# Two program jumps moved to the ends, LayerNorm roots on VectorE instead of ScalarE, and one MLP input taken off GpSimd

## The chip, the cores and the metric

The kernel runs on one core of one Trainium2 chip. The metric is the time of the whole program on the device, in microseconds (us), lower is better. The kernel before takes 1396.98 us (median of 3 runs, 1396.61 to 1397.05).

Words used here: TensorE does the matmuls, VectorE and ScalarE the elementwise work (VectorE also moves results out of PSUM, such as those of the matmuls with V, in 256 operations of line 755: an eviction), GpSimd helps, and SyncE issues data transfers, as ScalarE can too. In profile lines these are PE, DVE, ACT, POOL and SP; a q behind a name (ACTq, SPq) marks transfers issued by that engine. PSUM is the memory that the matmuls write. The granted clock is the share of TensorE's full clock that the trace shows as granted; a half-clock spell is a stretch in which it is 0.5. A milestone is the start of the same matmul in several traces.

## The reference, cut to what matters

```python
mod = (silu(c) @ w_mod).reshape(..., 6, 1, -1);  sa, ca, ga, sb, cb, gb = mod...
h = layernorm(x) * (1 + ca) + sa
x = x + ga * A(h)          # A: q = h @ wq; softmax(q k^T / sqrt(128)) v; @ wo
h = layernorm(x) * (1 + cb) + sb
x = x + gb * B(h)          # B: layernorm, gelu(@ w1), shifts, @ w2, + h; layernorm, gelu(@ w3) @ w4, + x1
# x: 2048 x 640; 32 heads of 128, 2048 cached keys and values per head; w_mod 640 x 3840
# w1, w2: 640 x 640; w3: 640 x 1728; w4: 1728 x 640; all bf16
```

## The kernel before: the parts that matter

The rows are cut into four chunks of 512, counted 0 to 3 in the code. Attention is 128 steps (8 groups of 4 heads, in each group 4 chunks of 4 heads). A step is 16 score matmuls (line 727), exps on ScalarE (729), 16 times 4 matmuls with V (746), and the projection of the next step's q (659). After 128 steps comes a tail for the MLP.

A list scheduler in the kernel puts every operation into one list per engine by cost and priority; each engine then executes its own list strictly in order. So an operation that is late holds back what stands behind it on its engine (at the end of attention TensorE stood for 3.75 us behind one eviction, below). The program has a fast path and a general path, which runs only if a check fails. Each engine runs a few operations, then jumps over the general path to the rest of its list:

```python
    FIRST = {"PE": 3, "ACT": 5, "DVE": 0, "POOL": 7, "SP": 7}   # operations ahead of the jump
...
        for e, eng in names.items():
            hint = eng.mark_branch_hint_location()
            run(e, 0, self.FIRST[e])
            eng.br("fast").branch_hint(hint)
        es.close()
        general()
        nc.switch_bb("fast")
        for e, eng in names.items():
            run(e, self.FIRST[e], None)
```

The first LayerNorm, with roots on ScalarE (Ln, then Exp of -0.5 times it), and the loads of heads:

```python
    def ln1(ch, prio):
        g = ln_slot()
        xs = x0 if ch == 0 else load_x2(...) + load_x2(...)
        for a in (0, 2):
            for i in (a, a + 1):
                ln_stats(xs[i].ap, (xs[i],), g, i, prio, 0.0 if ch == 0 else 2000.0)
            rstd_act(g, a, a + 2, prio - 100, 0.0 if ch == 0 else 1500.0)
            for i in (a, a + 1):
                normed(xn[i].ap, xn[i], xs[i].ap, xs[i], g, i, False, prio - 1)
        # ... cut: the transposes, on TensorE for chunk 0, by transfers for the others
    def load_head(h):
        # ... cut: b, n, pr
        load_k(h, pr, (wm[2],) if h == 1 else (), from_slot(n))       # 4 transposing transfers
        load_v(h, pr + 1, gate=(wm[2],) if h == 1 else (), need=from_slot(n + 1))
```

The tail is a list of pieces in the order TensorE executes them. A is a part of w1, B a tile of w2, C a part of w3, D a tile of w4, WO the last output projection of attention, I3 the MLP input (the double LayerNorm) of chunk 3:

```python
    TAIL = ("A0 B0 B1 B2 A1 B3 WO B4 B5 A2 B6 I3 B7 B8 C0 B9 D0 D1 ... ").split()
    WOD, CH, I3D = -200, -300, 0     # VectorE priorities: evictions of WO, rest of the tail, I3
...
    def mlp_in(ch, prio):
        for a in (0, 2):
            pool = ch < NC - 2 or (ch == NC - 2 and a == 0)      # half of chunk 2 on GpSimd
            # rstd: ScalarE if pool, else eight tiny Newton operations on VectorE
            ...
                if pool:
                    scaled("POOL", ...); tt("POOL", ... mod_t[4] ...); tt("POOL", ... mod_t[3] ...)
                else:
                    P.op("DVE", ... scalar_tensor_tensor(x1 - mean, times mod_t[4]) ...)
```

## Time and profile before

| what | value |
|---|---|
| time, median | 1396.98 us |
| profiled span | 1396.2 us, mean granted clock 0.995 |
| TensorE busy | 1382.3 us, 99% |
| first q projection starts | 16.40 us |
| last step of attention gives way to the tail (A0) | 1208.68 us |

TensorE is busy nearly all the time, so the change can only work on what TensorE loses. From the page of the kernel before, the busy line, and then the shares of the chain that ended last:

```profile
PE 1382.3 (99%) x13128; PEld 942.0 (67%) x13128; DVE 539.8 (39%) x1380; ACT 1106.6 (79%) x1164; POOL 110.4 (8%) x96
...
PE 97%; DVE 2%; issue 1%; DMA 0%; SPq 0%; ACT 0%; ACTq 0%; POOL 0%; POOLq 0%
```

TensorE's own waits (columns: engine, tile and line that waited, what it waited for; total us, how often, the longest), the largest ones:

```profile
PE f_O L857 <- DVE f_OO L755: 3.7, 1, 3.7
PE f_O L553 <- DVE f_xn L510: 1.5, 2, 0.9
...
PE f_M L445 <- DMA f_W<-in_w_mod_dram: 0.6, 2, 0.3
PE f_O L746 <- DMA f_KV<-in_A_v_cache_dram: 0.5, 1, 0.5
```

Two places stand out. The first is the start. ScalarE's timeline (start, busy time, engine, line, operation, output and input; in brackets the idle time before it and what ended it):

```profile
4.70 0.18 ACT L435 ACTIVATE f_small<-f_M 128x5 f32<-128x5 f32 x1
10.68 0.38 ACTq L612 DMA_DIRECT2D f_KV<-in_w_mod_dram  x1
11.10 0.54 ACTq L582 DMA_DIRECT2D f_KV<-in_A_v_cache_dram  x1
11.69 0.20 ACT L483 ACTIVATE f_small<-f_small 128x2 f32<-128x2 f32 x1 [6.81 <-issue]
```

ScalarE does nothing from 4.88 to 10.68 and waits for nothing that the profile shows: this is its jump. (The w_mod slice that its next load awaits landed only at 6.61, so the jump costs it about 4.1 us of these 5.8.) The first LayerNorm root (line 483) is late by that, and with it the first projection.

The second is the end of attention. VectorE's, GpSimd's and TensorE's timelines around it:

```profile
1203.49 1.48 DVE L496 SCALAR_TENSOR_TENSOR f_small<-f_small 128x2 f32<-128x2 f32 x1
1205.01 1.47 DVE L497 TENSOR_TENSOR f_small<-f_small 128x2 f32<-128x2 f32 x1
1206.51 1.47 DVE L498 SCALAR_TENSOR_TENSOR f_small<-f_small 128x2 f32<-128x2 f32 x1
1208.01 2.92 DVE L794 SCALAR_TENSOR_TENSOR f_y<-f_y,f_small,f_mod 128x640 f32<-128x640 f32 x2
...
1203.42 6.04 POOL L517 TENSOR_TENSOR f_y<-f_y,f_mod 128x640 f32<-128x640 f32 x4
...
1209.76 1.24 PE L857 MATMUL f_S<-f_wq,f_W 128*128 128x512 bf16 x5
1214.75 2.32 PE L857 MATMUL f_O<-f_wq,f_W 128*128 128x512 bf16 x5 [3.75 <-DVE f_OO L755]
```

Operations on 128 by 2 numbers, of 0.15 to 0.17 us elsewhere, take about as long as one of the GpSimd operations beside them (6.04 / 4 = 1.51 us). VectorE is late, TensorE waits 3.75 us for an eviction, and the next five matmuls take 2.32 us instead of 1.24, at half clock. Busy times in windows, with the granted clock behind the engines' columns (DMA share and GB/s last), for the two places:

```profile
15.00:20.00 5.00, 4.36 (x19) 1.98 (x17) 2.27 (x6) 1.45 (x2) 0.00 (x0) 0.51 1.36 183
...
1215.00:1220.00 5.00, 5.00 (x13) 1.82 (x12) 3.87 (x16) 1.20 (x2) 0.00 (x0) 0.50 0.49 81
```

### The profile page before, as it was taken

To read this page: it belongs to the slowest core of one execution; us is meant where nothing else is said; L and a number is where in the kernel's file an instruction comes from. 1 tells how busy PE (TensorE), PEld (TensorE's weight loads), DVE (VectorE), ACT (ScalarE), POOL (GpSimd) and SP (SyncE) were. 2 spreads that over 40 slices of the span, in tenths; PEclk is the share of its full clock that TensorE was granted. 3 is DMA by queue.
4 is the path that set the end of the run, shared out by engine and by line. 5 is a ranking of instruction groups with operands and counts; after the bars stand their busy time and mean duration, and the time that the engine had idled before them with its cause. 6 is when DMAs were issued, how large, how long until landed. Compare 5 with 4: busy or idle time off the path is not lost.

```text
span 1396.2 us, 29870 instructions
## 1 busy us (share of the span) xinstructions
PE 1382.3 (99%) x13128; PEld 942.0 (67%) x13128; DVE 539.8 (39%) x1380; ACT 1106.6 (79%) x1164; POOL 110.4 (8%) x96
## 2 busy tenths in 40 slices
PE   8999999999999999999999999999999999899999
PEld 6667767677777777777776777777776676555554
DVE  4452332333233322333233323333233345887653
ACT  4988888888888898888888888888888888643222
POOL 0000000000000000000000000001333248300000
PEclk9999999999999999999999999999999999999999
DMA  9661623161214321241206112612254112432110
GB/s 207 138 119 25 121 76 86 35 107 36 46 35 81 61 46 35 50 92 31 50 19 97 32 42 35 107 35 47 54 103 102 16 16 53 93 70 38 39 48 24
DMA packets 259180, 88.90 MB, mean 64 GB/s; under 512 B 236706, under 2 KB 257763, under 8 KB 259043
## 3 DMA queue, kind: packets, MB, share of 16 engines
q1 hardware_dynamic: 255762, 84.59, 30.8%
q10 hardware_dynamic: 3280, 2.33, 0.6%
q8 instruction: 105, 1.72, 0.6%
q14 instruction: 33, 0.26, 0.1%
HBM read 43.48 MB, written 2.62 MB: 33 GB/s over the span
## 4 chain that ended last, share of the span: by engine, by line
PE 97%; DVE 2%; issue 1%; DMA 0%; SPq 0%; ACT 0%; ACTq 0%; POOL 0%; POOLq 0%
PE f_O L746 33%; PE f_S L727 31%; PE f_M L659 10%; PE f_M L684 10%; PE f_M L921 3%; PE f_O L907 2%; PE f_S L907 2%; PE f_S L921 2%; PE f_S L880 1%; PE f_O L857 1%; PE f_S L857 1%; PE f_M L880 1%; DMA f_KV<-in_A_v_cache_dram 0%; PE f_M L604 0%; PE f_S L420 0%
## 5 line engine op out<-in xcount | busy, mean ns | idle before, releaser
L729 ACT ACTIVATE f_PQ<-f_S 128x1024 bf16<-128x1024 f32 x1024 | 1041.2, 1023 | 147.0 <-PE f_S L727 133.8
L746 PEld LDWEIGHTS f_O<-f_KV,f_PQ 128*128 128x128 bf16 x8192 | 589.5, 98 | 232.3 <-DVE f_OO L755 2.2
L727 PE MATMUL f_S<-f_PQ,f_KV 128*128 128x512 bf16 x2048 | 727.9, 380 | 0.5 <-ACT f_PQ L729 0.5
L746 PE MATMUL f_O<-f_KV,f_PQ 128*128 128x129 bf16 x8192 | 713.7, 220 | 1.4 <-DVE f_OO L755 0.9
L692 DVE TENSOR_TENSOR f_y<-f_M,f_y 128x320 f32<-128x320 f32 x192 | 94.4, 492 | 536.3 <-PE f_M L684 536.3
L684 PE MATMUL f_M<-f_wo,f_OO 128*128 128x320 bf16 x992 | 273.3, 300 | 0.0
L727 PEld LDWEIGHTS f_S<-f_PQ,f_KV 128*128 128x128 bf16 x2048 | 196.9, 98 | 30.7 <-ACT f_PQ L729 1.0
L659 PE MATMUL f_M<-f_hT,f_wq 128*128 128x512 bf16 x640 | 177.4, 381 | 1.1 <-DVE f_hT L562 0.6
L517 POOL TENSOR_TENSOR f_y<-f_y,f_mod 128x640 f32<-128x640 f32 x36 | 55.6, 1557 | 820.1 <-DVE f_y L692 819.9
L684 PEld LDWEIGHTS f_M<-f_wo,f_OO 128*128 128x128 bf16 x992 | 96.1, 98 | 28.5
L755 DVE TENSOR_TENSOR f_OO<-f_O,f_rl 128x256 bf16<-128x256 f32 x256 | 108.5, 424 | 8.2
L662 DVE CAST f_PQ<-f_M 128x512 bf16<-128x512 f32 x128 | 88.5, 692 | 56.2 <-PE f_M L659 56.0
L659 PEld LDWEIGHTS f_M<-f_hT,f_wq 128*128 128x128 bf16 x640 | 62.2, 98 | 65.9 <-DVE f_hT L562 1.6
L753 DVE RECIPROCAL f_rl<-f_O 128x2 f32<-128x2 f32 x256 | 43.4, 170 | 32.4 <-PE f_O L746 28.2
L910 ACT ACTIVATE f_OO<-f_S 128x512 bf16<-128x512 f32 x28 | 16.7, 597 | 39.6 <-PE f_S L907 39.6
L690 DVE COPY f_y<-f_M 128x320 f32<-128x320 f32 x32 | 15.7, 490 | 62.4 <-PE f_M L684 62.4
L921 PE MATMUL f_M<-f_KV,f_OO 128*128 128x320 bf16 x252 | 38.6, 301 | 0.0
L921 PEld LDWEIGHTS f_M<-f_KV,f_OO 128*128 128x128 bf16 x252 | 23.2, 97 | 15.6 <-issue 6.0
L523 ACT ACTIVATE f_xn<-f_y,f_small 128x640 bf16<-128x640 f32 x10 | 9.1, 914 | 29.6 <-DVE f_small L502 29.6
L478 DVE BATCH_NORM_STATS2 f_small<-f_y 128x6 f32<-128x320 f32 x64 | 29.8, 479 | 2.0 <-POOL f_y L517 2.0
L921 PE MATMUL f_S<-f_KV,f_OO 128*128 128x320 bf16 x196 | 30.0, 301 | 0.0
L910 ACT ACTIVATE f_OO<-f_O 128x512 bf16<-128x512 f32 (+1 forms) x28 | 16.6, 594 | 12.0 <-PE f_O L907 12.0
(136 smaller groups left out, 521.1 us busy)
## 6 DMA issues: line engine op xcount, KB each, us to landing
f_KV<-in_A_v_cache_dram SPq DMA_DIRECT2D x31, 512.0 KB, 4.6
f_wo<-in_A_wo_dram SPq DMA_DIRECT2D x8, 640.0 KB, 4.3
f_xin<-in_A_x_dram SPq DMA_DIRECT2D x15, 320.0 KB, 3.6
f_wq<-in_A_wq_dram SPq DMA_DIRECT2D x7, 640.0 KB, 4.6
f_W<-in_w_mod_dram SPq DMA_DIRECT2D x3, 800.0 KB, 4.8
out_dram<-f_xin SPq DMA_DIRECT2D x15, 160.0 KB, 1.8
f_KV<-in_B_w_dram SPq DMA_DIRECT2D x5, 432.0 KB, 3.4
f_KV<-in_A_k_cache_dram SPq DMA_TRANSPOSE x128, 3.0
```

The lines of the kernel that those rows point to most:

```text
L517: P.op(eng, lambda e: e.tensor_tensor(out=out, in0=a, in1=b, op=op), COST[eng][0], rd, wr, prio, lat=300 if eng == "POOL" else None)
L659: P.op("PE", lambda e, i=i, kk=kk: e.matmul(m.ap, wq_t[g % 2][:, kk, hh * 128:(hh + 1) * 128], hT_t[ch][:, kk, :], start=(i == 0), stop=(i ...
L662: P.op("DVE", lambda e: e.tensor_copy(q.ap, m.ap), 690, (m,), (q,), s * NP - 90)
L684: P.op("PE", lambda e, m=m, qt=qt, hf=hf, hh=hh: e.matmul(m[:, 0:HD], OT_ap[gs][:, qt, hh, :], wo_t[g % 2][:, hh, hf * HD:(hf + 1) * HD], ...
L692: P.op("DVE", lambda e, m=m, yt=yt: e.tensor_tensor(out=yt.ap, in0=m[:, 0:HD], in1=yt.ap, op=ALU.add), 490, (m, yt), (yt,), s * NP - 60)
L727: P.op("PE", lambda e, sp=sp, r=r, kt=kt: e.matmul(sp[:, r * QC:(r + 1) * QC], K_ap[b][:, kt * 128:(kt + 1) * 128], q.ap, start=True, stop ...
L729: x = P.op("ACT", lambda e, sp=sp, pt=pt: e.activation(pt.ap.rearrange("p k q -> p (k q)"), sp.ap, ACT.Exp, scale=SCALE), 1021, (sp,), (pt ...
L746: ins = e.matmul(o[bk][:, w * 129:w * 129 + 129], pt[:, r, qt * 128:(qt + 1) * 128], V_ap[b][:, u, 0:129], start=(u == 0 and w == 0), stop ...
L753: P.op("DVE", lambda e, ov=ov, i0=i0: e.reciprocal(rl_t[:, i0:i0 + 2].unsqueeze(2), ov[:, 0:258].rearrange("p (u d) -> p u d", u=2)[:, :, ...
L755: evac.append(P.op("DVE", lambda e, ov=ov, i0=i0, bk=bk: e.tensor_tensor(out=On_ap[gs][:, 2 * bk:2 * bk + 2, hh, :], in0=ov[:, 0:258].rear ...
L907: P.op("PE", lambda e, m=m, f=f, kk=kk, fs=fs: e.matmul(m[0:fs, :], w3_ap[:, kk, f * 128:f * 128 + fs], nT_ap[ch][:, kk, :], start=(kk == ...
L921: P.op("PE", lambda e, f=f, hf=hf, fs=fs: e.matmul(m[:, hf * 512:hf * 512 + HD], gT_ap[0:fs, f, i * 128:(i + 1) * 128], w4_ap[f][0:fs, hf ...
```

## The change

The intent: ScalarE and SyncE no longer pay for their jump at the start; the roots of later chunks' first LayerNorm go to VectorE as Newton iterations, off the busy ScalarE; and the MLP input of chunk 2 (the third) no longer uses GpSimd, so that VectorE is not slowed at the end of attention. The tail's order and priorities are tuned anew.

```diff
-    FIRST = {"PE": 3, "ACT": 5, "DVE": 0, "POOL": 7, "SP": 7}
+    FIRST = {"PE": 3, "ACT": 10000, "DVE": 0, "POOL": 7, "SP": -5}
+    HINT = {"PE": 0, "ACT": -30, "DVE": 0, "POOL": 0, "SP": -12}
...
         for e, eng in names.items():
+            n = self.HINT[e] % len(self.seq[e])
+            run(e, 0, n)
             hint = eng.mark_branch_hint_location()
-            run(e, 0, self.FIRST[e])
+            run(e, n, self.FIRST[e])
             eng.br("fast").branch_hint(hint)
... ln1:
-        for a in (0, 2):
+        for a, z in ((0, 2), (2, 4)) if ch < 2 else ((0, 4),):
...
-            rstd_act(g, a, a + 2, prio - 100, 0.0 if ch == 0 else 1500.0)
+            if ch == 0:
+                rstd_act(g, a, z, prio - 100)
+            else:
+                rstd_dve(g, a, z, prio - 1)
... tail:
-    TAIL = ("A0 B0 B1 B2 A1 B3 WO B4 B5 A2 B6 I3 B7 B8 C0 B9 D0 D1 D2 D3 C1 D4 A3 B10 B11 "
-            "B12 B13 B14 D5 D6 D7 B15 C2 D8 D9 D10 D11 C3 D12 D13 D14 D15").split()
+    TAIL = ("A0 B0 B1 A1 B2 B3 WO B4 B5 I3 A2 B6 C0 B7 D0 D1 D2 B8 D3 B9 C1 D4 A3 B10 B11 "
+            "B12 D5 B13 D6 B14 D7 B15 C2 D8 D9 D10 D11 C3 D12 D13 D14 D15").split()
-    WOD, CH, I3D = -200, -300, 0
+    QUAD = (2, 3)
+    WOD, CH, I3D = -100, -1000, -200
... mlp_in:
-        for a in (0, 2):
-            pool = ch < NC - 2 or (ch == NC - 2 and a == 0)
+        pool = ch < NC - 2
+        for a, z in ((0, 4),) if ch in QUAD else ((0, 2), (2, 4)):
... (the rest follows from a, a + 2 becoming a, z, and cost entries 825 becoming 890)
```

More of the change, by code (lines that the diff above doesn't have):

```diff
@@ L536, in ln1 @@
         xs = x0 if ch == 0 else load_x2(4 * ch, XP[ch], from_slot(XS[ch])) + load_x2(4 * ch + 2, XP[ch], from_slot(XS[ch]))
-        for a in (0, 2):
-            for i in (a, a + 1):
+        for a, z in ((0, 2), (2, 4)) if ch < 2 else ((0, 4),):
+            for i in range(a, z):
                 ln_stats(xs[i].ap, (xs[i],), g, i, prio, 0.0 if ch == 0 else 2000.0)
-            rstd_act(g, a, a + 2, prio - 100, 0.0 if ch == 0 else 1500.0)
-            for i in (a, a + 1):
+            if ch == 0:
+                rstd_act(g, a, z, prio - 100)
+            else:
+                rstd_dve(g, a, z, prio - 1)
+            for i in range(a, z):
                 normed(xn[i].ap, xn[i], xs[i].ap, xs[i], g, i, False, prio - 1)
@@ L771, in rstd @@
                 if pool:
-                    rstd_act(g, a, a + 2, prio, 2000.0)
-                    negate(g, a, a + 2, prio, 2000.0)
-                else:
-                    rstd_dve(g, a, a + 2, prio)
-            for i in (a, a + 1):
+                    rstd_act(g, a, z, prio, 2000.0)
+                    negate(g, a, z, prio, 2000.0)
+                else:
+                    rstd_dve(g, a, z, prio)
+            for i in range(a, z):
                 t = ch * 4 + i
@@ L779, in mlp_in @@
             if not pool:
-                for i in (a, a + 1):
+                for i in range(a, z):
                     t = ch * 4 + i
@@ L783, in mlp_in @@
                         out=b.ap, in0=x1[t].ap, scalar=mv_ap[g1][:, i, 0:1], in1=mod_t[4][:], op0=ALU.subtract, op1=ALU.mult),
-                        825, (x1[t], mvs[g1][i]) + tuple(mod[4]), (xb[t],), prio)
+                        890, (x1[t], mvs[g1][i]) + tuple(mod[4]), (xb[t],), prio)
             rstd(g1)
-            for i in (a, a + 1):
+            for i in range(a, z):
                 t = ch * 4 + i
@@ L795, in mlp_in @@
                         out=b.ap, in0=b.ap, scalar=rs_ap[g1][:, i:i + 1], in1=mod_t[3][:], op0=ALU.mult, op1=ALU.add),
-                        825, (b, rs[g1]) + tuple(mod[3]), (b,), prio)
+                        890, (b, rs[g1]) + tuple(mod[3]), (b,), prio)
                 ln_stats(b.ap, (b,), g2, i, prio, 500.0)
@@ L799, in mlp_in @@
             if tail:
-                shift(g2, a, a + 2, prio)
-            for i in (a, a + 1):
+                shift(g2, a, z, prio)
+            for i in range(a, z):
                 t = ch * 4 + i
```

## The prediction

> **What bounds the kernel now.** TensorE: 99% busy on the page and 97% of the chain of waits. The change touches only the two ends, so I account for TensorE's lost time there.
>
> *Start.* The timeline shows ScalarE idle from 4.88 to 10.68 us; the chain of waits calls 5.92 us of it "issue". That is its jump after five operations; the w_mod slice that its next DMA awaits landed at 6.6. The delay holds the first LayerNorm root (11.69), so the first projection starts at 16.40. SyncE's jump delays the second K transpose to about 13.9, though its gate landed at 9.96. TensorE idles meanwhile, and the clock is halved from 15.1 to 21.9 (0.51 in the window 15 to 20). [...]
>
> *Tail.* At 1211.0 TensorE waits 3.75 us for a VectorE eviction (L755), its longest wait. VectorE was behind: tiny Newton operations took 1.48 us instead of 0.16, and L794 1.46 instead of 0.88, while GpSimd ran its 1.5 us tensor operations of chunk 2's MLP input (1203.4 to 1209.4). The gap cools the clock: half from 1213.1 to 1220.0, about 2.7 us of work lost (five matmuls take 2.3 us, not 1.24). [...]
>
> **What the change does.**
> 1. ScalarE issues its DMAs at 6.6, its first root about 8.1. Then wm slices, not ScalarE, bound TensorE: the third lands at 9.96 and now competes with 1.3 MB issued 4 us earlier. First projection about 14.8: 1.6 us gained. [...] Expected 2.8.
> 2. Roots by Newton cost VectorE eight operations of about 0.1 us per pair, off the critical path. The new order puts the eviction ahead of the cast that delayed TensorE at 32.3 to 33.4 (about 0.7), and the waits near 50 (0.7) mostly go. Expected 1.2.
> 3. Tail: no GpSimd beside VectorE, so the 3.75 us wait and its half clock go: 6.4. One GELU wait (0.28) goes.
> 4. Cost: VectorE takes two more tiles (about 4.6 us), repaid by the contention that ends. Step 126's eviction now stands behind four 0.8 us operations (about 0.5 lost), and the last output projection's evictions stand behind LayerNorm work, so its fifth and seventh groups should wait for PSUM, about 1.5 us against 0.45 before. A possible cold window there: 0.6 on average. Other slips 0.4. Together 2.6.
> 5. The late jumps: ScalarE's after its last GELU, SyncE's before the last five stores: hidden.
>
> Sum: 2.8 + 1.2 + 6.7 - 2.6 = 8.1 us. Predicted 1389, eight times in ten within 1384 to 1394. Faster by over 2%: 0.005; within 2%: 0.99; slower: 0.005.
>
> **What would show it.** Timeline: ScalarE's first Ln near 8, first projection near 14.8; clock row full at 15 to 25 or not (step 1's coin). TensorE's waits: no 3.75 us for L755; clock full at 1205 to 1225; Newton operations all near 0.15 us; a wait of 1 to 2 us in the last output projection. Middle steps unchanged.
>
> **What would make it wrong.** The early 1.3 MB delaying w_mod or K; the clock going cold anyway; a late jump landing on the end; the tail's VectorE queue holding back the first w3 tile.

The sum: 2.8 + 1.2 + 6.7 - 2.6 = 8.1 us. Cut from the forecast are two sentences that rest on general rules and not on a trace of this case, and in item 1 the sentence that took 1.6 to 2.8: the other 1.2 us were the author's estimate for a chance, put at 55%, that the half-clock spell at the start would stay away ("step 1's coin"). Without it the terms come to 6.9 us. A cold spell or cold window is a half-clock spell; its 0.6 in item 4 is a bet on its coming, like the 55%. The Newton operations of item 2, put there at about 0.1 us, take 0.11 to 0.17 us in the changed kernel (0.16 mostly; 28.06 to 33.8 us).

## The result, and the profile after

The changed kernel takes 1392.62 us (median of 4 runs, 1391.46 to 1392.70), where the kernel before took 1397.01 (1396.61 to 1398.72, 4 runs) in the same rounds. The ratio is 0.9964, 95% interval 0.9947 to 0.9982: the same within 2%. Ratios here and below are the mean time of one kernel's fast runs over the mean of the other's fast runs of the same rounds, so not quite the ratio of the medians. In means the kernel won 5.0 us (1397.34 to 1392.35), where the prediction had said 8.1.

The changed kernel's line numbers are 3 to 7 higher: 746 is now 753, 659 is 666, 684 is 691, 445 is 448, 755 is 762, 794 is 801. TensorE's waits after:

```profile
PE f_O L753 <- DMA f_KV<-in_A_v_cache_dram: 1.9, 1, 1.9
PE f_O L691 <- DVE f_tmp L702: 1.4, 1, 1.4
PE f_M L448 <- issue: 1.3, 1, 1.3
...
PE f_O L691 <- DVE f_small L500: 0.5, 1, 0.5
```

The wait of 3.7 us is gone; a wait for V of a head, 0.5 us before, is now 1.9; the last output projection (line 691) waits 2.0 us in all, 0.45 before; and there is a pause of 1.3 us marked issue. ScalarE at the start, and TensorE's pause as the chain of waits shows it:

```profile
7.18 0.39 ACTq L618 DMA_DIRECT2D f_KV<-in_w_mod_dram  x1
...
8.62 0.20 ACT L486 ACTIVATE f_small<-f_small 128x2 f32<-128x2 f32 x1 [3.21 <-DVE f_small L482]
...
11.91 0.13 PE f_M L448 x6
12.03 1.34 issue
13.38 0.25 PE f_M L448 x4
```

The jump is gone from ScalarE's start: its first root begins at 8.62 instead of 11.69. The tail's output projection, where TensorE now loses time (its timeline), and the clock there and at the start (windows):

```profile
1225.74 0.71 PE L691 MATMUL f_S<-f_wo,f_OO 128*128 128x320 bf16 x4
1227.88 0.72 PE L691 MATMUL f_O<-f_wo,f_OO 128*128 128x320 bf16 x4 [1.43 <-DVE f_tmp L702]
...
1229.67 1.25 PE L691 MATMUL f_O<-f_wo,f_OO 128*128 128x320 bf16 x4 [0.54 <-DVE f_small L500]
...
15.00:20.00 5.00, 5.00 (x20) 2.14 (x20) 2.37 (x5) 1.86 (x4) 0.13 (x1) 0.71 1.29 224
...
1230.00:1235.00 5.00, 5.00 (x28) 3.11 (x27) 2.99 (x11) 0.11 (x1) 0.00 (x0) 0.70 0.32 64
```

Where the time went is read best from milestones: the start times, in us, of the same matmuls in both traces.

| TensorE reaches | before | after | gain so far |
|---|---|---|---|
| first q projection | 16.40 | 14.85 | 1.55 |
| second | 22.84 | 20.26 | 2.58 |
| third | 31.02 | 28.44 | 2.58 |
| fourth | 39.94 | 36.61 | 3.33 |
| fifth | 48.11 | 44.91 | 3.20 |
| sixth | 57.57 | 55.84 | 1.73 |
| A0, first part of w1 | 1208.68 | 1207.44 | 1.24 |
| last output projection (WO) | 1232.30 | 1224.12 | 8.18 |
| A2, third part of w1 | 1239.98 | 1235.12 | 4.86 |
| D15, last tile | 1389.04 | 1384.17 | 4.87 |

(Up to WO and up to A2 TensorE does the same work in both, in a slightly different order.) Four things happen. The start gains 2.6 us. Of 3.3 us in hand at the fourth projection, 1.6 are gone at the sixth. The end of attention and the first tiles gain 6.9. The output projection gives 3.3 back. After A2 nothing changes.

### The profile page after: what moved, and what is told of

It reads as the page before. It is cut to its first block, busy times and chain, and to the rows that moved or that the text cites. A ratio compares the mean times of both kernels' runs of the same rounds, so it can differ in the third digit from the quotient of the medians.

```text
span 1391.3 us, 29861 instructions
## 1 busy us (share of the span) xinstructions
PE 1379.4 (99%) x13128; PEld 941.2 (68%) x13128; DVE 539.6 (39%) x1401; ACT 1101.5 (79%) x1143; POOL 100.9 (7%) x88
## 4 chain that ended last, share of the span: by engine, by line
PE 97%; DVE 1%; DMA 1%; SPq 0%; issue 0%; ACT 0%
PE f_O L753 33%; PE f_S L734 31%; PE f_M L666 10%; PE f_M L691 10%; PE f_M L928 3%; PE f_S L914 2%; PE f_O L914 2%; PE f_S L928 2%; PE f_S L887 1%; PE f_S L864 1%; PE f_O L864 1%; PE f_M L887 1%; DMA f_W<-in_w_mod_dram 0%; DMA f_KV<-in_A_v_cache_dram 0%; SPq L573 0%; PE f_M L610 0%
## 5 line engine op out<-in xcount | busy, mean ns | idle before, releaser
L520 POOL TENSOR_TENSOR f_y<-f_y,f_mod 128x640 f32<-128x640 f32 x32 | 49.6, 1560 | 820.1 <-DVE f_y L699 819.9
L928 PE MATMUL f_M<-f_KV,f_OO 128*128 128x320 bf16 (+1 forms) x308 | 47.1, 300 | 0.0
L928 PEld LDWEIGHTS f_M<-f_KV,f_OO 128*128 128x128 bf16 (+1 forms) x308 | 28.6, 97 | 18.7 <-issue 7.0
L917 ACT ACTIVATE f_OO<-f_S 128x512 bf16<-128x512 f32 (+1 forms) x28 | 16.7, 595 | 13.1 <-PE f_S L914 13.1
L942 DVE TENSOR_TENSOR f_y<-f_M,f_y 128x640 f32<-128x640 f32 x10 | 8.2, 825 | 43.2 <-PE f_M L928 43.2
```

Source lines behind the costliest of these rows:

```text
L520: P.op(eng, lambda e: e.tensor_tensor(out=out, in0=a, in1=b, op=op), COST[eng][0], rd, wr, prio, lat=300 if eng == "POOL" else None)
L928: P.op("PE", lambda e, f=f, hf=hf, fs=fs: e.matmul(m[:, hf * 512:hf * 512 + HD], gT_ap[0:fs, f, i * 128:(i + 1) * 128], w4_ap[f][0:fs, hf ...
```

## The experiments

Twelve kernels were run. Single times differ from launch to launch (the kernel before alone took 1393.14 to 1399.68 in eleven runs on one chip), so runs taken once are read by their milestones. In five traces (act_only, sp_only, tail_only, pool_short, both_align) some 1.8% of the matmul records are missing; their milestones were found by the order of lines, and differences between them agree to a few hundredths where nothing was changed.

| run | ScalarE's first root | first projection | V of head 3 issued | sixth projection | wait for that V | A0 to A2 | half clock in the tail |
|---|---|---|---|---|---|---|---|
| before | 11.69 | 16.40 | 46.24 | 57.57 | 0.5 | 31.30 | 6.83 us at 1213 |
| act_only | 8.09 | 18.96 | 45.11 | 57.96 | none | 31.54 | 6.83 at 1214 |
| sp_only | 12.31 | 17.66 | 47.66 | 59.02 | 1.1 | 31.26 | 6.83 at 1214 |
| pool_short | 12.80 | 18.15 | 47.37 | 58.49 | 0.6 | 24.81 | none |
| tail_only | 11.00 | 16.14 | 46.03 | 57.30 | 1.7 | 26.05 | none |
| after | 8.62 | 14.85 | 44.35 | 55.84 | 1.9 | 27.68 | 3.41 at 1230 |
| after_again | 7.76 | 15.50 | 44.78 | 56.20 | 1.9 | 27.73 | 3.41 at 1230 |
| pe_align | 8.07 | 16.33 | 43.15 | 54.86 | none | 26.06 | none |
| ln_act | 7.79 | 16.65 | 43.73 | 55.55 | none | 26.06 | none |
| pe_jump2 | 8.10 | 19.48 | 43.75 | 56.64 | none | 26.05 | none |
| v3_act | 7.76 | 16.10 | 36.27 | 54.42 | none | 26.06 | none |
| b4_wo | 7.76 | 15.82 | 44.02 | 55.31 | 0.5 | 25.19 | none |
| both | 7.93 | 14.47 | 35.05 | 54.32 | none | 25.21 | none |
| both_align | 8.52 | 14.66 | 34.02 | 55.79 | none | 25.21 | none |

### The two jumps alone, each on the kernel before

act_only, on the kernel before:

```diff
-    FIRST = {"PE": 3, "ACT": 5, "DVE": 0, "POOL": 7, "SP": 7}
+    FIRST = {"PE": 3, "ACT": 10000, "DVE": 0, "POOL": 7, "SP": 7}
+    HINT = {"PE": 0, "ACT": -30, "DVE": 0, "POOL": 0, "SP": 0}
```

> The kernel before with ScalarE's jump alone moved to its end. Theory [...]: ScalarE issues its next DMA at about 7 us, its first Ln stands near 8.5, the first projection starts near 14.9 instead of 16.40, as in the changed kernel; TensorE shows an unexplained pause of over 1 us near 12 to 13.4 [...], because it gets there earlier. SyncE's second K transpose stays near 14. Rival (ScalarE only waited for the w_mod slice or for VectorE's statistics): first Ln stays near 11.7 and the first projection near 16.4. Whole time 1 to 3 us under the kernel before.

Measured: 1398.14 us (the kernel before 1394.91 on that chip, both once, at mean clocks of 0.995 and 1.000, so the two times say little). ScalarE's first root came at 8.09, 3.6 us earlier, as in the changed kernel. But TensorE's first projection started at 18.96. Its waits show why:

```profile
PE f_M L448 <- issue: 4.1, 1, 4.1
```

TensorE paused for 4.1 us that the profile puts on no other engine, at the same matmul at which the changed kernel paused 1.3.

sp_only, on the kernel before:

```diff
-    FIRST = {"PE": 3, "ACT": 5, "DVE": 0, "POOL": 7, "SP": 7}
+    FIRST = {"PE": 3, "ACT": 5, "DVE": 0, "POOL": 7, "SP": -5}
+    HINT = {"PE": 0, "ACT": 0, "DVE": 0, "POOL": 0, "SP": -12}
```

> The kernel before with SyncE's jump alone moved late. Theory: the second K transpose is issued near 9.5 to 10.5 instead of 14, but the first projection stays near 16.4, since ScalarE's jump holds it; the V load of head 3 (second last SyncE issue before the output projection's weights) comes 2 to 4 us earlier than 46.24, so the small TensorE wait for it (0.5 us) goes. Rival (SyncE's jump is what delays the first projection): first projection near 15. Whole time within 1.5 us of the kernel before.

Measured: 1398.9 us (1394.91). SyncE's second K transpose came at 9.54 instead of 14.04, and still V of head 3 was issued at 47.66, later than in the kernel before. SyncE's list did not run faster, since its transposes took longer. TensorE waited 1.13 us for this V, and 1.37 us for V of head 0 too, which ScalarE had issued as late as before (11.16) and which landed at 25.40 instead of 19.28. SyncE's timeline of sp_only:

```profile
16.05 10.98 SPq L580 DMA_TRANSPOSE f_KV<-in_A_k_cache_dram  x4
```

The same four of head 1 took 5.06 us in the kernel before and 6.45 in the changed one. What follows from both: the two jumps do remove the delay they were meant to remove, but neither part alone gains, as other limits stand close behind. Single runs of the start differ by 2 us, so no small loss is claimed either.

### The tail alone, and GpSimd alone

tail_only is the changed kernel's tail (order, priorities, quads, no GpSimd for chunk 2) with the jumps early and all roots of the first LayerNorm on ScalarE, as in the kernel before:

```diff
 # on the changed kernel
-    FIRST = {"PE": 3, "ACT": 10000, "DVE": 0, "POOL": 7, "SP": -5}
-    HINT = {"PE": 0, "ACT": -30, "DVE": 0, "POOL": 0, "SP": -12}
+    FIRST = {"PE": 3, "ACT": 5, "DVE": 0, "POOL": 7, "SP": 7}
+    HINT = {"PE": 0, "ACT": 0, "DVE": 0, "POOL": 0, "SP": 0}
...
-        for a, z in ((0, 2), (2, 4)) if ch < 2 else ((0, 4),):
+        for a, z in ((0, 2), (2, 4)):
...
... (the two branches for ch == 0 and the rest become one line)
+            rstd_act(g, a, z, prio - 100, 0.0 if ch == 0 else 1500.0)   # for every chunk
```

> The changed kernel with both jumps early again and the roots of later chunks back on ScalarE: only the tail of the change is left. Theory (the two ends add up independently): first projection near 16.4 as in the kernel before, the step before the tail begins as in the kernel before (within 0.5 us), no long wait for the eviction at the tail's start, first w2 tile about 7 us earlier than before, waits of 1.4 and 0.5 us in the last output projection. Whole time 3 to 6 us under before, depending on whether the clock goes cold in the output projection. Rival (the tail's gain comes from the start being earlier): whole time within 1.5 us of before.

Measured: 1392.48 us (1394.91). A0 to A2 took 26.05 us, against 31.30 before: 5.25 us, which is the tail's worth. It is more than the 3.62 that the changed kernel's own trace showed, because there was no half clock in the output projection this time, although the same two waits were there (2.0 us together).

pool_short, on the kernel before (relative error 0.159): GpSimd's four operations of chunk 2 touch 8 columns instead of 640. Its output is wrong, which doesn't matter for the time. The lists of all engines stay as they were.

```diff
-                    tt("POOL", b.ap, b.ap, mod_t[4][:], ALU.mult, ...)
-                    tt("POOL", b.ap, b.ap, mod_t[3][:], ALU.add, ...)
+                    w = 8 if ch == NC - 2 else D
+                    tt("POOL", b.ap[:, 0:w], b.ap[:, 0:w], mod_t[4][:, 0:w], ALU.mult, ...)
+                    tt("POOL", b.ap[:, 0:w], b.ap[:, 0:w], mod_t[3][:, 0:w], ALU.add, ...)
```

> The kernel before, wrong result on purpose: the four GpSimd tensor operations of chunk 2's MLP input work on 8 columns instead of 640; the order of every engine is unchanged. Theory (VectorE was slowed by GpSimd's work beside it): the Newton operations take 0.15 to 0.2 us again instead of 1.48, the modulation operations 0.88 instead of 1.46, VectorE reaches the last eviction near 1209, the 3.75 us TensorE wait shrinks to under 0.5, the clock stays full there, whole time 5 to 7 us under before. Rival (the eviction stands too late in VectorE's order, whatever GpSimd does): the wait stays over 2 us and the clock goes cold again.

Measured: 1391.92 us (1394.91). Timelines of GpSimd, VectorE and TensorE in pool_short:

```profile
1204.34 0.69 POOL L517 TENSOR_TENSOR f_y<-f_y,f_mod 128x8 f32<-128x8 f32 x4
...
1204.41 0.16 DVE L496 SCALAR_TENSOR_TENSOR f_small<-f_small 128x2 f32<-128x2 f32 x1
1204.61 0.16 DVE L497 TENSOR_TENSOR f_small<-f_small 128x2 f32<-128x2 f32 x1
...
1211.76 1.24 PE L858 MATMUL f_O<-f_wq,f_W 128*128 128x512 bf16 x5
```

With GpSimd's operations short, VectorE's tiny operations are back at 0.16 us, the wait of 3.75 us and its half clock are gone, and A0 to A2 takes 24.81 us. Nothing in VectorE's order had changed, so the wait came from GpSimd working beside VectorE, as the prediction said, and not from the order of VectorE's list. How GpSimd's work slows VectorE (from 0.16 to 1.48 us) no run shows.

### V of head 3: SyncE's list, or the transfers?

SyncE is never idle between its second K transpose and the issue of this V, the 32nd entry of its list. From the one to the other it took 32.20 us in the kernel before (14.04 to 46.24) and 34.82 in the changed one (9.53 to 44.35): of 4.5 us gained, 1.9 are left. In the seven traces where V goes through SyncE and TensorE waits for it, the sixth projection starts 11.1 to 11.5 us after V's issue, whatever the first projection did. SyncE's timeline in the changed kernel, towards V:

```profile
31.92 5.03 SPq L583 DMA_TRANSPOSE f_KV<-in_A_k_cache_dram  x3
36.99 6.01 SPq L573 DMA_TRANSPOSE f_hT<-f_xn  x4
43.04 1.26 SPq L583 DMA_TRANSPOSE f_KV<-in_A_k_cache_dram  x1
44.35 0.58 SPq L588 DMA_DIRECT2D f_KV<-in_A_v_cache_dram  x1
```

v3_act sends that one load through ScalarE:

```diff
-        load_v(h, pr + 1, gate=(wm[2],) if h == 1 else (), need=from_slot(n + 1))
+        load_v(h, pr + 1, "ACT" if h == 3 else "SP", gate=(wm[2],) if h == 1 else (), need=from_slot(15 if h == 3 else n + 1))
```

> The changed kernel with one line moved: the load of head 3's V goes through ScalarE's DMA queue, gated on the 16th exp, instead of SyncE's, where it stands 32nd. In all six traces so far in which TensorE waits for this V, the sixth q_proj starts 11.1 to 11.5 us after V's issue. Theory (SyncE is issue bound, so V is late): V is issued near 36 to 40 us instead of 44.35, TensorE's wait for f_KV from in_A_v_cache (1.9 us) is gone, and from the fifth to the sixth q_proj it takes 8.2 to 9.2 us instead of 10.93; nothing else moves: the time falls by 1.4 to 2.7 against a run with the same start. Rival (the 16 DMA engines are full of transposes, so V is late whoever issues it): the wait stays at 1 us or more and the stretch at 10 us or more.

Measured: 1389.6 us (the kernel before 1395.16 on that chip, both once). V was issued at 36.27 and had landed by 41.71; the fifth to the sixth projection took 8.37 us instead of 10.93; the view of TensorE's waits lists none from 20 to 60 us. The theory's prediction holds, but the run tells less than hoped: pe_align and ln_act, with V through SyncE, show no wait for V either, because their first projections came at 16.3 and 16.7. With almost the same start as pe_align (16.10 and 16.33) v3_act reaches the sixth projection only 0.4 us earlier. V is late only for a kernel that is early. The run both (below), with a start as early as the changed kernel's, settles it. It was issue time that was short here: the transfer itself took 4.69 us through SyncE (44.35 to 49.04) and 5.4 through ScalarE, so it was not faster, only issued 8 us sooner.

### The roots on VectorE

ln_act puts the roots of chunks 1 to 3 back on ScalarE, in pairs, and leaves the rest of the change:

```diff
-        for a, z in ((0, 2), (2, 4)) if ch < 2 else ((0, 4),):
+        for a, z in ((0, 2), (2, 4)):
...
-            if ch == 0:
-                rstd_act(g, a, z, prio - 100)
-            else:
-                rstd_dve(g, a, z, prio - 1)
+            rstd_act(g, a, z, prio - 100, 0.0 if ch == 0 else 1500.0)
```

> The changed kernel with only the LayerNorm roots of chunks 1 to 3 put back on ScalarE, in pairs. Theory: Newton on VectorE is worth 0.75 us once, because the evictions of the third head then stand ahead of a cast: from the third to the fourth q_proj this run takes 8.9 us as the kernel before did, not 8.17, and the wait for V grows or shrinks by what comes before it, so that at the sixth q_proj at most 0.3 us of the 0.75 is left; total change within 0.6 us. Rival: the roots on VectorE are worth 1 us or more, or cost something, which then shows at the sixth q_proj or later.

Measured: 1390.75 us (1395.16). From the third to the fourth projection it takes 8.92 us, as in the kernel before and in every run with these roots on ScalarE; the changed kernel takes 8.17. So Newton on VectorE is worth 0.75 us there, once, by letting an eviction stand ahead of a cast. Beyond the sixth projection nothing differs except step 126, where both lose the same: from the sixth projection to A0 the changed kernel and ln_act take 1151.60 us, the kernel before 1151.11.

### The output projection and its half clock

b4_wo moves the output projection one tile back and its evictions ahead of the LayerNorm work on VectorE:

```diff
-    TAIL = ("A0 B0 B1 A1 B2 B3 WO B4 B5 I3 ...
+    TAIL = ("A0 B0 B1 A1 B2 B3 B4 WO B5 I3 ...
-    WOD, CH, I3D = -100, -1000, -200
+    WOD, CH, I3D = -1050, -1000, -200
```

> The changed kernel with the last output projection behind w2 tile 4 instead of before it, and its evictions at priority -1050 (ahead of the late chunks' LayerNorm) instead of -100. Theory (its evictions stand behind LayerNorm work on VectorE, and the gap[...] costs about 2.9 us of what the tail gained): the two waits of 1.4 and 0.5 us in the output projection shrink to 0.4 to 0.9 together, no half clock near 1230, and from the first w1 part to the third (A0 to A2) it takes 25.0 to 26.9 us instead of 27.68 (before 31.30). Rival (the half clock falls there anyway[...]): the clock row shows half clock between 1225 and 1240 again, and A0 to A2 stays at 27.2 or more.

Measured: 1389.63 us (1395.16). The output projection waits 0.5 us in all, A0 to A2 takes 25.19 us, no half clock. Since ln_act, v3_act, pe_jump2 and pe_align, which keep the changed kernel's order, take 26.06 us without half clock, b4_wo's edit is worth 0.87 us, and the half clock 1.65 us where it comes (27.71, the mean of the two traces with it, less 26.06).

after_again is the changed kernel, unaltered, in five rounds.

> The changed kernel once more, unaltered, as the measure for the two runs beside it and to see whether its half clock near 1230 comes back. Four traces with the same tail order (tail_only, v3_act, ln_act, pe_jump2) took 26.05 us from the first w1 part to the third, without half clock there; the first trace of the changed kernel took 27.68 with it. Theory [...]: 26.05 again more likely than not. Rival (the cold spell belongs to this kernel): 27.7 again with half clock. The time: 3.5 to 6.5 us below the kernel before in the same rounds. The pause of TensorE after its 181st matmul comes again, 1.3 to 3.0 us.

Measured: 1391.46 us median (1390.03 to 1393.56, 6 runs), the kernel before 1396.12 (1393.14 to 1399.68, 11 runs), ratio 0.9962 (0.9948 to 0.9977). The half clock near 1230 came back. Windows of after_again, then of v3_act, which has the same order in the tail and the same waits of 1.42 and 0.54 us:

```profile
1230.00:1235.00 5.00, 4.95 (x25) 3.04 (x25) 2.95 (x10) 0.00 (x0) 0.00 (x0) 0.66 0.34 67
```

```profile
1230.00:1235.00 5.00, 5.00 (x31) 2.84 (x30) 4.62 (x15) 2.08 (x3) 0.00 (x0) 1.00 0.32 64
```

So seven traces with this order and these waits (tail_only among them) show it twice. The ten timed runs of the changed kernel fit that: five have a mean granted clock of 0.997 or 0.998 and take 1392.91 us on average, five have 0.999 or 1.0 and take 1391.11. (That the lower clock of those runs is the same spell is an inference: two spells of 3.41 us at half clock lower the mean by 0.0025.) The half-clock spells in the two traces of the pair last 3.413 us each in the changed kernel (14.48 to 17.89 and 1229.62 to 1233.03) and 6.827 us each in the kernel before, and from the start of the first to the start of the second it is 1215.14 us in the changed kernel, 1198.08 in the kernel before and 1201.49 in sp_only. The three distances are 356, 351 and 352 times one step of 3.4133 us (an estimate: each distance divided by that whole number; the shorter spells are as long as one step). Where such a step falls relative to TensorE's two waits differs from trace to trace, and the seven traces fit one reading. Counted in steps of 3.4133 us from each trace's first half-clock spell, the two waits (1.97 us together) fall into one step, with 1.91 and 1.97 us of them, in the two traces with half clock; in the other five no step holds more than 1.79 us of them. By this reading the loss is luck. (No limit on the idle time alone comes out of the traces: elsewhere 1.59 us in one step was followed by half clock, in both_align at 43.5 us, and 1.73 us was not, in tail_only at 48.6 us.)

The kernel before has such luck too. Its 22 timed runs beside after_again and both_align have mean clocks from 0.995 (5 runs, 1398.7 us on average) to 0.999 (4 runs, 1394.7 us). Its profiled run, with two spells of 6.83 us, is one of 0.995, so it is at the slow end. Which spell is missing in the faster runs no trace shows.

### The pause of TensorE at the start

Counting matmuls from the start of the program shows that the pause always follows the 181st, in all kernels with ScalarE's late jump and TensorE's jump after three operations: the 182nd starts 1.5 (after), 2.1 (after_again), 2.8 (v3_act), 3.0 (ln_act), 2.4 (b4_wo), 2.6 (pe_align), 0.8 (both) and 4.2 us (act_only) after it. The records of transfers show a packet of 16,384 bytes of instructions at that time (such packets number 105 in the whole trace, for 26,571 recorded instructions of TensorE, so about 253 to each; that they are TensorE's is inferred from this): in the changed kernel it starts at 10.90, takes 1.12 us, and TensorE resumes at 13.38; in act_only it starts at 13.94, takes 1.15, and TensorE resumes at 16.51. In the kernel before, the packet starts at 11.31, no earlier, but there TensorE waits for VectorE until 12.66, and the pause after the 181st matmul is only 0.19 us: in this pair of traces the pause comes from TensorE getting there sooner, not from a later packet. That TensorE waits for this packet is inference.

pe_jump2 tests this by moving TensorE's jump, which changes how many instructions lie ahead of this matmul. (The theory is that the pause goes from the 181st matmul when code is shifted.)

```diff
-    FIRST = {"PE": 3, "ACT": 10000, "DVE": 0, "POOL": 7, "SP": -5}
+    FIRST = {"PE": 2, "ACT": 10000, "DVE": 0, "POOL": 7, "SP": -5}
```

> The changed kernel with TensorE's jump over the general path one operation earlier (two operations in the first block instead of three, the second warm-up spin behind the jump). TensorE pauses 1.34 us at 12.0 to 13.4 in the changed kernel[...]. Theory [...]: with the jump earlier [...]the pause at this place shrinks to below 0.5 us; the first projection starts at 13.3 to 14.2. Rival 1 (the w_mod slices would hold it anyway, as the prediction said): the pause is replaced by waits for w_mod and the first projection stays at 14.5 to 15.1. Rival 2 [...]: a pause of over 1 us marked issue turns up at another place, or the warm-up spin starts late.

Measured: 1391.8 us (1395.16). The pause at the 181st matmul went, but a longer one came after the 54th, in the warm-up:

```profile
PE f_S L423 <- issue: 4.8, 1, 4.8
```

This is the second rival. The run has a use of its own: its first projection starts 4.6 us later than the changed kernel's (19.48), and its sixth only 0.8 us later (56.64). Most of what the start wins or loses is levelled out by then: of the 3.8 us caught up, 2.75 fall between the fifth and the sixth projection, where the changed kernel waits for V, and 0.95 between the first and the second, where it ran at half clock (14.48 to 17.89) and pe_jump2 did not.

pe_align was to shift the addresses of TensorE's fast path by 200 no-operations in the general path.

```diff
         es.close()
+        for _ in range(200):
+            nc.tensor.nop()
         general()
```

> The changed kernel with 200 no-operations put into TensorE's program ahead of the general path, where the fast path never executes them: they only shift the addresses of the fast path's code. TensorE's pause has come after its 181st matmul in every trace with ScalarE's late jump and with TensorE's jump after three operations (1.5 to 4.2 us between the starts of the 181st and the 182nd, at 11.9 to 12.3), 96 matmuls or 192 instructions behind the jump. Theory [...]: the pause leaves the 181st matmul[...]; the first projection starts near 13.4 and the time falls by 1 to 2.5 us unless the wait for V takes it back (then 0 to 0.7). Rival 1: the pause stays at the 181st (the place is set by the data, not by addresses). Rival 2: the pause moves to the 209th with its full length.

Measured: 1390.59 us median (1390.03 to 1391.31, 4 runs) against 1396.12 for the kernel before. The pause stayed after the 181st matmul, 2.6 us. That would have been the first rival, but the compiled program has no no-operations in it: TensorE's list is the same as the changed kernel's, and the run is only a repeat of it. It says nothing of addresses.

both_align does it with instructions that stay in the program, 100 matmuls in the general path, which is not executed. It was put on both, the version below.

```diff
                     W(t, e_dw, 16)
+                    for _ in range(100):
+                        t.matmul(QPp[:, 0:128], s_bc[:, 0, :], wmod[:, 0, 0:128], start=True, stop=True)
```

> The run both with 100 matmuls (200 instructions of TensorE) added to the general path, which is not executed: a second try at what pe_align was for, since the no-operations of pe_align turned out not to be in its program at all (TensorE's instruction list is the same as the changed kernel's, so pe_align was only a repeat, and says nothing of addresses). This time they are in the list. They only shift the addresses of TensorE's fast path. Theory [...]: no pause after the 181st matmul (0.8 to 4.2 us in eight traces); [...]the first projection starts at 13.3 to 13.8 (14.47 in both, 14.85 to 18.96 in the others); the time is 0 to 2 us below the 1388.6 of both, so 1386.5 to 1388.5 where the kernel before takes 1396. Rival 1: the pause stays at the 181st matmul (it is set by the data, not by addresses). Rival 2: it moves to the 209th with 1 us or more, and nothing is gained.

Measured: no pause after the 181st matmul nor at the 209th (where the second rival expected it: an estimate, 56 instructions further, about the 253 of a packet less the 200 put in), so the pause did hang on addresses (in this one trace, where eight others had it) and the first rival falls. An instruction packet came at 11.10 all the same, but no pause followed it. And nothing was gained: the first projection starts at 14.66, and the sixth at 55.79. TensorE's waits up to 60 us in both_align:

```profile
PE f_M L665 <- DVE f_hT L575: 1.6, 2, 1.3
PE f_M L665 <- DVE f_hT L568: 1.1, 1, 1.1
PE f_M L448 <- DMA f_W<-in_w_mod_dram: 0.6, 1, 0.6
```

The pause is replaced by waits for a w_mod slice, for chunk 0's normalised rows (line 568, 1.1 instead of 0.6) and for chunk 1's (line 575). The time is 1390.33 us median (1387.78 to 1391.60, 6 runs), ratio 0.9951 (0.9939 to 0.9963) to its own runs of the kernel before, so it is no better than both. Part of the profiled run's late sixth projection is the clock: after the wait of 1.3 us for line 575, from 43.96 to 45.30, it ran at half clock from 46.91 to 50.33, which both did not. Why the packet comes as late as 10.66 to 13.94 in the traces with the pause is open: other transfers are under way at that time (the view of windows gives a DMA share of 1.03 for 10 to 15 us in the changed kernel), but no run shows whether they delay it.

### A version that beats both kernels

both has the edits of v3_act and b4_wo together.

```diff
-    TAIL = ("A0 B0 B1 A1 B2 B3 WO B4 B5 I3 ...
+    TAIL = ("A0 B0 B1 A1 B2 B3 B4 WO B5 I3 ...
-    WOD, CH, I3D = -100, -1000, -200
+    WOD, CH, I3D = -1050, -1000, -200
...
-        load_v(h, pr + 1, gate=(wm[2],) if h == 1 else (), need=from_slot(n + 1))
+        load_v(h, pr + 1, "ACT" if h == 3 else "SP", gate=(wm[2],) if h == 1 else (), need=from_slot(15 if h == 3 else n + 1))
```

> The changed kernel with the two edits that helped put together: V of head 3 through ScalarE's queue (as v3_act), and the last output projection behind w2 tile 4 with its evictions at -1050 (as b4_wo). Theory (they act at different ends, so they add): no wait for V, the fifth to the sixth q_proj in 8.2 to 8.6 us, A0 to A2 in 25.2 us; 2.0 to 4.0 us below the changed kernel of the same rounds, about 1388 on a chip where the kernel before takes 1395. Rival (what is gained at the start is lost at a later wait): less than 1.5 us below.

Measured: 1388.58 us median (1387.92 to 1390.64, 6 runs), in the same rounds as after_again's 1391.46 and the kernel before's 1396.12; ratio 0.9943 (0.9929 to 0.9957) to the kernel before, where after_again has 0.9962. In means of these rounds both is 3.0 us faster than the changed kernel (1388.81 and 1391.79) and 7.9 faster than the kernel before (1396.71). Its first projection starts at 14.47, close to the changed kernel's 14.85, and with V early the sixth starts at 54.32 instead of 55.84, although a new wait of 1.2 us (for a Newton operation on VectorE, at 30 us) has come between. The start is not quite the same, as both had no half clock there and the changed kernel had 3.41 us of it, but that lead was lost to the new wait: the two stand level at the fourth projection (36.66 and 36.61). From there to the sixth both takes 17.66 us, the changed kernel 19.23. That is the fair test of V: from the same place, the wait of 1.9 us is gone with SyncE out of the way (one trace of both). Its output projection:

```profile
1226.38 0.72 PE L690 MATMUL f_O<-f_wo,f_OO 128*128 128x320 bf16 x4
...
1228.18 0.72 PE L690 MATMUL f_O<-f_wo,f_OO 128*128 128x320 bf16 x4 [0.54 <-DVE f_tmp L701]
```

## Why the prediction was right or wrong, point by point

The time, 1392.62 us, lies inside the predicted range of 1384 to 1394, and within 2% was the likeliest class. The centre, 1389.0, was 3.6 us too low. Term by term, from the first pair of traces:

| term, as predicted | predicted gain | measured | where read |
|---|---|---|---|
| 1. ScalarE's jump, with the clock | 2.8 | 2.6 | second projection |
| 2. Newton roots, the order, the waits near 50 | 1.2 | -0.85 | second to sixth projection |
| 3. the tail's wait, its half clock, a GELU wait | 6.7 | 6.9 | A0 to WO |
| 4. step 126, the output projection, a cold spell, slips | -2.6 | -3.8 | sixth to A0 (-0.5), WO to A2 (-3.3) |
| sum | 8.1 | 4.9 | end |

**The step that failed is in item 2: "the waits near 50 (0.7) mostly go".** The other half of that item was right: an eviction now goes ahead of a cast, worth 0.75 us (8.17 instead of 8.92 from the third to the fourth projection; ln_act takes it back). But the wait for V of head 3 grew from 0.5 to 1.9 us. I had taken what the start gains as gained to the end. It was not: V is the 32nd entry of SyncE's list, SyncE works without a gap from 10 to 48 us, and its transposes took longer when they started earlier (the four of head 1 5.06 us before, 6.45 after), so V's issue moved by 1.9 us where TensorE's fourth projection had moved by 3.3. TensorE then waits for what it gained. sp_only, pe_jump2 and both show this from three sides: starting SyncE 4.5 us earlier did not issue V earlier, starting TensorE 4.6 us later cost only 0.8 us at the sixth projection, and taking V off SyncE's list ended the wait.

**Item 1 had the right number for a wrong reason, by luck.** The prediction said 14.8 for the first projection because "wm slices, not ScalarE, bound TensorE" and would suffer from the 1.3 MB issued 4 us earlier. The projection came at 14.85, but the third and the fifth slice landed earlier than before (9.51 and 10.42 us, against 9.96 and 10.85; the fourth 0.3 us later), and TensorE waited 0.4 us for w_mod in all, 0.6 before. TensorE paused after its 181st matmul instead, marked issue, 1.34 us in this trace and 0.6 to 4.1 us in others; the same kernel, run again, started its first projection at 15.50. Without that pause the first projection would have started between 13.5 and 13.9 in the traces with the change's two late jumps and the pause (an estimate: the start less the pause), and both_align shows that other waits would then have taken most of it. The clock's coin fell half way: half clock for 3.41 us instead of 6.83.

**Item 3 was right in cause, and in size for this pair of traces.** The 3.75 us wait and its half clock went, the Newton operations take 0.15 to 0.17 us, and pool_short shows that GpSimd beside VectorE made the wait. The kernel before's trace has the full half clock of 6.83 us there; by the mean clocks of its timed runs, many have less half clock in all, so the average gain may be smaller than 6.9.

**Item 4 had the right mechanisms and was too small in one term.** Step 126's eviction cost 0.49 us (0.5 predicted). The output projection's fifth and seventh groups wait as predicted, 1.43 and 0.54 us against 0.45 before. The cold spell was put at 0.6 us on average; it costs 1.65 when it comes, came in both traces of the changed kernel and, by their clocks, in about half of its ten timed runs, so its average is near 0.8, and the first trace happened to have it.

**Item 5, the late jumps hidden, held.** From A2 to the end both kernels take the same time (154.76 us before, 154.75 after, to the last issue of the fast path).

The warnings named the early 1.3 MB delaying w_mod or K. K's transposes were indeed slower on SyncE (6.45 us instead of 5.06 for the four of head 1), but it was V, behind them in the list, that TensorE came to wait for. The scatter of about half a per cent between launches, from the start's pause and from the half-clock spells, is as large as the miss of any one term; the centre's miss of 3.6 us is mostly item 2 (2.0) and item 4 (1.2).

## What to carry to other kernels

Time won at the start of a long pipeline is kept only up to the next in-order list that did not move: before counting it, follow every list, SyncE's above all, up to the first item that TensorE needs and ask by how much that item moves. GpSimd work beside tiny VectorE operations can make each of them as long as the GpSimd operation (1.48 us instead of 0.16 here), so keep it away from places where VectorE holds the last eviction. Where two waits of 1.4 and 0.5 us stand close together, as here, a half-clock spell can come in some of the runs and not in others (two of seven traces), so judge by several traces, of the kernel before as well.
